# Query and key projections on column strips of TensorE, without padded weight copies

## The chip, the cores and the metric

The kernel runs on one core of a Trainium2 chip. A core has a matrix engine (TensorE, PE in the profile; its weight loads are listed apart as PEld), a vector engine (VectorE, DVE), an engine for functions of one variable (ScalarE, ACT), a general engine (GpSimd, POOL) and an engine that only issues transfers (SyncE, SP). Each works through its own list of instructions in order, and they wait for each other by semaphores. Operands lie in SBUF, 128 partitions wide; matmuls write to PSUM, eight banks of 128 x 512 fp32 numbers, from which DVE or ACT has to fetch the result ("evict" it). The metric is device time in microseconds (us), the median over several executions.

## The reference

Two layers are applied to x (2048 tokens, 448 features, bf16). Each is an attention block followed by a mixing block with an MLP, both on a normalised input:

```
qkv = layernorm(x) @ wqkv                 # 16 heads of 28 features each for q, k and v
p   = softmax(q @ k.T * 28**-0.5)
x   = x + (p @ v) @ wo
h   = gelu(layernorm(x') @ w1)            # x' = layernorm(x)
x1  = x' + shifted(h) @ w2                # four groups of features shifted by -1, +1, -2, +2 tokens
x   = x + x1 + gelu(layernorm(x1) @ w3) @ w4
```

Both layers share all weights.

## The kernel before

**Layout.** A head has 28 features, but TensorE's strips are 32 wide. So four heads form a group g (0 to 3) of 128 rows: head j of the group lies in rows 32j to 32j+27, and the four rows behind it hold helpers. `kT` and `qT` are kept in this way, transposed, with tokens along the free axis. Row 28 and row 29 of each head carry a bound on the scores, so that the exponential can run without a running maximum: rows 28 and 29 of K are 1 (the column `MK` adds them at eviction); row 28 of Q takes a multiple of the squared norm of the query, scaled by `ACOL`, and row 29 of Q a bias from the largest key norm. `ACOL` and `RTN` come from the norms of the weights themselves, which `wnorm` works out at the start: squares of the weights, column sums with a matmul by ones (L761), and sums over each head with a matmul by `astat` (L766).

**Weights of q and k.** `t_setup` loads them into `wst`, pieces of the later MLP buffer `h2T`, 112 features x 4 chunks x 448 columns. `pad_cast` then copies them to `wk_pad` and `wq_pad`, with each head's 28 columns at a multiple of 32 and zeros between: a copy for group 0 and two copies for groups 1 to 3, for each of the two (ACT at L741, or DVE at L743). `wnorm` squares the padded copies (ACT at L753, DVE at L755).

**Projections.** `kq_proj` makes 128 rows of K or Q for up to 512 tokens: four matmuls, one for each chunk of 112 features, with 128 padded columns as weights (L662); an eviction to `kT` or `qT` with a number as factor and, for K and later Q units, a column as addend (L930 to L937); squares of the result (L941, L943); and a matmul by `astat` that sums the squares over each head. `mm` gives every such matmul a second form, four matmuls on strips of 32 output columns (L665), which the planner takes when TensorE is already working in strips.

**Order.** Nothing is issued in the order of the source. Generators yield operations to a planner (`Sched`), which has a table of durations, due times from earlier rounds, and lists of seeds (`MOVES`) that disturb the due times at given points. It writes out a fixed order for every engine, and fills holes of TensorE with matmuls of ones (L1695). TensorE works in one of three tilings: scores on strips of 32 rows (L1252), products with V on strips of 32 columns (L1327, L665), and whole (L662, L872, L1695).

**Attention.** The scores of two or three blocks of 128 x 512 at a time (L1252) go through one exponential on ACT (L1278) of 1024 or 1536 columns; some blocks are taken to DVE instead (L1168 to L1181). The results meet V at L1327. Two score buffers of three banks alternate, so the scores of a step need the exponential two steps back. From the first exponential on, ACT is reserved for them, beside the tanh of the mixer (L1442) and the gelu of the MLP in nine batches (L1659). The first layer's projections of later tokens, the mixer, the MLP and the second layer's projections are laid between the scores. ACT evicts projections only before the first exponential.

Of the kernel before, what the change touches and what calls it, by code (L numbers as in the profile page):

```python
# [496 lines left out]
def build_kernel(nc, A_x, A_wqkv, A_wo, B_x, B_w1, B_w2, B_w3, B_w4, out, n_layers=2):  # L497
    S = A_x.shape[1]
    D = 448
# [21 lines left out]
            (0.00, 453789), (16.37, 681098), (32.56, 797911), (48.59, 756531), (64.60, 616122), (96.69, 243454), (112.73, 402327), (129.20, 347222),  # L521
            (193.55, 37042), (210.08, 918064), (242.29, 341149), (258.31, 397655), (274.47, 223313), (290.49, 246614), (306.70, 234581), (322.77, 119869),
            (338.97, 396652), (355.15, 335807), (391.48, 966107), (440.04, 112069), (520.56, 389665), (536.62, 623460), (552.63, 145884), (568.71, 985658),
            (584.75, 199060), (600.79, 794212), (620.06, 440366), (668.32, 428831), (700.60, 742412), (717.08, 172111), (733.21, 350167), (781.36, 465123),
            (797.48, 750518), (829.75, 99856), (845.88, 932005), (881.89, 550401), (898.03, 280990), (914.20, 779388), (946.64, 938909), (962.75, 215389),
            (978.81, 470403), (999.69, 102110), (1015.80, 600949), (1031.80, 257283),
        ],
        [
            (0.00, 913344), (12.07, 790630), (36.26, 358045), (48.38, 33421), (72.46, 243766), (96.67, 865488), (108.71, 222308), (145.54, 574177),
            (169.92, 505472), (194.21, 959135), (206.41, 140361), (218.93, 663650), (231.06, 874019), (255.76, 124206), (291.86, 733013), (328.10, 30459),  # L530
            (340.32, 970941), (364.69, 337305), (413.00, 152706), (425.18, 488991), (437.30, 939877), (449.57, 988047), (461.65, 669914), (473.72, 905087),
            (486.00, 87997), (498.03, 41039), (510.11, 162929), (522.19, 860735), (534.22, 735239), (546.27, 581631), (558.30, 115844), (570.45, 436555),
            (582.65, 408875), (606.74, 311018), (642.89, 325568), (667.19, 827655), (679.29, 868524), (691.61, 820707), (703.87, 927266), (716.12, 142611),
            (728.33, 661842), (752.69, 290694), (764.79, 914552), (776.96, 336386), (789.12, 558591), (801.16, 794121), (825.52, 153383), (849.92, 859691),
            (866.07, 319846), (878.17, 724156), (902.44, 789185), (914.49, 528957), (950.68, 252067), (974.81, 692424), (987.77, 461824), (1011.86, 320288),
            (1023.89, 587050), (1035.91, 787182), (1048.10, 662426),
# [40 lines left out]
    def c_act(n):  # L577
        return 0.08 + n * 0.000833
# [5 lines left out]
    with st:  # L584
        def sb(name, shape, dt):
            return st.enter_context(nc.sbuf_tensor(name, shape, dt))
# [25 lines left out]
        wq_pad = sb("wq_pad", [128, 4, 512], BF16)  # L612
        wk_pad = sb("wk_pad", [128, 4, 512], BF16)
# [32 lines left out]
        MK = cols[:, 4:5]  # L646
        ACOL, RTN, TMP, T2 = (sc[:, i, :] for i in range(4))
# [9 lines left out]
        def op(eng, dur, fn, reads=(), writes=(), **kw):  # L657
            return (eng, dur, fn, list(reads), list(writes), kw)
# [11 lines left out]
        def alt(eng, dur, fn, **kw):  # L670
            return (eng, dur, fn, kw)
# [17 lines left out]
        def t_setup():  # L689
            xin = A_x[0].rearrange("(t p) d -> p t d", p=128)  # L690
            wst = [h2T[:, 0:4, 0:D], h2T[:, 4:8, 0:D], wv]
            pads = ((wk_pad, "wk_pad"), (wq_pad, "wq_pad"))
# [5 lines left out]
            def ld_w(ci):  # L698
                return op("sp", 0.1, lambda e: e.dma_start(out=wst[ci][0:112, :, :], in_=A_wqkv[:, ci * D:(ci + 1) * D].rearrange("(c p) n -> p c n", p=112)),
                          writes=[("wst", ci)], dma=True, dma_time=(7.4, 6.4, 5.0)[ci])  # L700
# [15 lines left out]
            for (wp, nm) in pads:  # L716
                yield op("dve", 0.2, lambda e, wp=wp: e.memset(wp[:, :, :].rearrange("p c (h r) -> p c h r", r=32)[:, :, :, 28:32], 0.0), writes=[(nm, 0), (nm, 1)])
# [5 lines left out]
            yield op("dve", 0.15, lambda e: e.tensor_tensor(out=MK, in0=M28, in1=M29, op=ALU.add), reads=[("cols",)], writes=[(("cols",), 4)])  # L723
            yield ("sig", ("setup0",))
# [6 lines left out]
            def pad_cast(i, s):  # L731
                nm = pads[i][1]
                h0, h1 = ((0, 4), (4, 16))[s]
                nh = h1 - h0
                args = [(pads[i][0][0:112, :, 32 * h0:32 * h1].rearrange("p c (h r) -> p c h r", r=32)[:, :, :, 0:DH],
                         wst[1 - i][0:112, :, DH * h0:DH * h1].rearrange("p c (h r) -> p c h r", r=DH))]
                if s == 1:
                    args = [(a[:, 2 * k:2 * k + 2], z[:, 2 * k:2 * k + 2]) for a, z in args for k in range(2)]
                for k, (a, z) in enumerate(args):
                    n = 4 * DH * nh // len(args)  # L740
                    yield op("act", c_act(n), lambda e, a=a, z=z: e.activation(out=a, in_=z, func=ACT.Identity),  # L741
                             reads=[("wst", 1 - i)], writes=[((nm, s), k)],
                             alt=[alt("dve", c_b2b(n) + 0.1, lambda e, a=a, z=z: e.tensor_copy(out=a, in_=z))])  # L743

            def wnorm(s):
                gs = ((0,), (1, 2, 3))[s]
                ng = len(gs)
                lo, o = 128 * gs[0], 2 * gs[0]
# [3 lines left out]
                for i in range(2):  # L752
                    yield op("act", c_act(512 * ng), lambda e, i=i: e.activation(out=wsqs[i][0:112, :, lo:lo + 128 * ng], in_=pads[i][0][0:112, :, lo:lo + 128 * ng], func=ACT.Square),  # L753
                             reads=[(pads[i][1], s)], writes=[keys[i]],
                             alt=[alt("dve", c_f2b(512 * ng), lambda e, i=i: e.tensor_tensor(out=wsqs[i][0:112, :, lo:lo + 128 * ng], in0=pads[i][0][0:112, :, lo:lo + 128 * ng],  # L755
                                                                                            in1=pads[i][0][0:112, :, lo:lo + 128 * ng], op=ALU.mult))])
                b = yield ("acq", MISC, keys)
                for i in range(2):
                    for k, g in enumerate(gs):
                        for fc in range(4):  # L760
                            yield op("pe", 0.06, lambda e, fc=fc, i=i, k=k, g=g, b=b: e.matmul(  # L761
                                out=ps[:, bi(b), ng * i + k:ng * i + k + 1], lhsT=wsqs[i][0:112, fc, 128 * g:128 * g + 128], rhs=ones_bf[0:112, 0:1],
                                start=(fc == 0), stop=(fc == 3)),
                                reads=[keys[i], ("ones_bf",)], writes=[(("ps", bi(b)), ("c", i, g))], touch=[b])
                yield op("dve", 0.1, lambda e, b=b: e.tensor_copy(out=csum[:, o:o + 2 * ng], in_=ps[:, bi(b), 0:2 * ng]), reads=[("ps", bi(b))], writes=[("csum", s)], touch=[b])
                yield op("pe", 0.06, lambda e, b=b: e.matmul(out=ps[:, bi(b), 16:16 + 2 * ng], lhsT=astat[:, :], rhs=csum[:, o:o + 2 * ng], start=True, stop=True),  # L766
                         reads=[("csum", s), ("astat",)], writes=[(("ps", bi(b)), "h")], touch=[b])
# [17 lines left out]
            yield from pad_cast(0, 0)  # L785
            yield from pad_cast(1, 0)
# [3 lines left out]
            yield from pad_cast(0, 1)  # L790
            yield from pad_cast(1, 1)
# [131 lines left out]
        def kq_proj(xt, g, wpad, wnm, dst, dkeys, bias, bkey, nw, mul):  # L923
            b = yield ("acq", MISC, [xt.key, (wnm, min(g, 1))])
            for (fc, rows) in KCM:
                yield mm(nw, 128, lambda a, z, b=b: ps[a:z, bi(b), 0:nw], lambda a, z, fc=fc, rows=rows: wpad[0:rows, fc, 128 * g + a:128 * g + z],
                    xt.v[0:rows, 0:nw // 128, fc, :], fc == 0, fc == 3,
                    reads=[xt.key, (wnm, min(g, 1))], writes=[("ps", bi(b))], touch=[b])
            if bias is None:
                yield op("dve", 0.06 + c_ps(nw), lambda e, b=b: e.tensor_scalar(out=dst, in0=ps[:, bi(b), 0:nw], scalar1=mul, scalar2=None, op0=ALU.mult),  # L930
                         reads=[("ps", bi(b))], writes=dkeys, touch=[b],
                         alt=[alt("act", c_act(nw), lambda e, b=b: e.activation(out=dst, in_=ps[:, bi(b), 0:nw], func=ACT.Identity, scale=mul))])
            else:
                yield op("dve", 0.06 + c_ps(nw), lambda e, b=b: e.tensor_scalar(  # L934
                    out=dst, in0=ps[:, bi(b), 0:nw], scalar1=mul, scalar2=bias, op0=ALU.mult, op1=ALU.add),
                    reads=[("ps", bi(b)), bkey], writes=dkeys, touch=[b],
# [20 lines left out]
        def k_proj(L, c, g, xt):  # L957
            t0, n = KCH[L][c]
            c0, nw = kcol(L, t0), 128 * n
            b2 = yield from kq_proj(xt, g, wk_pad, "wk_pad", kT[:, g, c0:c0 + nw], [("kT", g, vslot(L, t0 + i)) for i in range(n)], MK, ("cols",), nw, 1.0)  # L960
# [5 lines left out]
        def q_proj(L, u, g, xt):  # L966
# [8 lines left out]
            b2 = yield from kq_proj(xt, g, wq_pad, "wq_pad", qt[:, g, q0:q0 + nw], wk, bias, bkey, nw, QS)  # L975
# [611 lines left out]
        def t_mixB(L, tiles, h0, batch, prio):  # L1587
# [18 lines left out]
            wstk = [("wst", 0), ("wst", 1), ("wsq",)]  # L1606
# [179 lines left out]
```

## Time and profile before

| what | value |
|---|---|
| median of 4 runs | 1063.4 us (1062.33 to 1066.47) |
| profiled execution | 1063.62 us |
| its span, first to last instruction | 1061.9 us |
| mean granted clock of TensorE | 0.995 |
| busy PE, ACT, DVE, POOL | 1023.4, 1016.2, 734.8, 58.8 us |
| matmuls in the trace | 9072 |
| first exponential, last exponential ends | 29.30, 1024.64 us |

A line of the timeline gives start and duration in us, engine, line of the source, operation, the tile written and the tiles read, shapes, how many instructions are merged in it, and in brackets how long the engine stood idle before and for whom. A line of a group gives the count after an x, the busy time, the mean duration in ns of one, and the idle time before them with what ended it. Durations of matmuls overlap: one of 512 columns lasts about 390 ns from end to end, but the next starts long before. So their pace is read from start to start.

### The profile page before, as it was taken

How to read it: one execution, taken by the hardware profiler on the slowest of the kernel's cores; microseconds unless marked ns; L12 is line 12 of the kernel's file. 1: busy time of each engine (PE TensorE's matmuls, PEld its weight loads, DVE VectorE, ACT ScalarE, POOL GpSimd, SP SyncE). 2: the span in 40 equal slices, each digit the busy share in tenths (PEclk: the TensorE clock that was granted, in tenths of full speed). 3: DMA queues.
4: the chain of work that ended last, by engine and by line, in shares of the span. 5: the costliest groups of instructions: out<-in, count | busy, mean ns of one | idle time of the engine just before them, and what ended most of it. 6: DMA issues, size and time to landing. Idle time of an engine off the chain costs nothing.

```text
span 1061.9 us, 21167 instructions
## 1 busy us (share of the span) xinstructions
PE 1023.4 (96%) x9072; PEld 398.1 (37%) x9072; DVE 734.8 (69%) x1685; ACT 1016.2 (96%) x938; POOL 58.8 (6%) x78
## 2 busy tenths in 40 slices
PE   9999999999999999999999999999999999999998
PEld 5333333333333333332343433333333333434455
DVE  7977478866887538887489656865869645665454
ACT  5999999999999999999999999999999999999983
POOL 1100000000000001010000000000011000010000
PEclk8999999999999999999999999999999999999999
DMA  4233141000001002100021002311010000000000
GB/s 115 60 111 100 35 122 20 2 16 20 21 1 21 1 1 41 35 21 1 21 41 31 26 15 77 90 31 40 21 36 2 20 14 19 22 21 2 15 6 23
DMA packets 70712, 35.04 MB, mean 33 GB/s; under 512 B 56473, under 2 KB 65049, under 8 KB 70617
## 3 DMA queue, kind: packets, MB, share of 16 engines
q1 hardware_dynamic: 70616, 33.68, 12.5%
q8 instruction: 71, 1.16, 0.4%
q14 instruction: 25, 0.20, 0.1%
HBM read 12.70 MB, written 7.08 MB: 19 GB/s over the span
## 4 chain that ended last, share of the span: by engine, by line
ACT 60%; PE 32%; DVE 5%; DMA 1%; issue 1%; POOL 0%; POOLq 0%; SPq 0%; DVEq 0%
ACT PT L1278 54%; PE ps L662 12%; PE ps L1252 8%; PE ps L1327 6%; ACT h2T L1659 4%; PE ps L1695 3%; PE ps L665 3%; ACT L1659 1%; DMA xT<-xn 1%; ACT gt L1442 1%; DMA h2T<-in_A_wqkv_dram 0%; ACT L1278 0%; DVE hT L1446 0%; DVE kT L934 0%; PE ps L872 0%
## 5 line engine op out<-in xcount | busy, mean ns | idle before, releaser
L1278 ACT ACTIVATE PT<-ps 128x1024 bf16<-128x1024 f32 (+1 forms) x821 | 916.7, 1221 | 10.0 <-PE ps L1252 6.9
L1252 PE MATMUL ps<-qT,kT 32*128 32x512 bf16 x1536 | 239.7, 384 | 11.7 <-ACT PT L1278 9.0
L1327 PE MATMUL ps<-PT,vaug 128*32 128x512 bf16 (+1 forms) x2253 | 233.6, 361 | 3.0 <-ACT PT L1278 1.9
L1695 PE MATMUL ps<-ones_bf 128*128 128x256 bf16 x1002 | 155.9, 280 | 2.0 <-DVE hot L696 1.1
L1252 PEld LDWEIGHTS ps<-qT,kT 32*128 32x128 bf16 x1536 | 58.8, 91 | 195.1 <-ACT PT L1278 104.9
L662 PE MATMUL ps<-xT,w 112*128 112x512 bf16 (+5 forms) x640 | 130.9, 327 | 0.8 <-DVE h2T L1618 0.6
L1695 PEld LDWEIGHTS ps<-ones_bf 128*128 128x128 bf16 x1002 | 83.5, 99 | 74.0 <-issue 55.2
L1618 DVE CAST h2T<-ps 128x512 bf16<-128x512 f32 (+2 forms) x126 | 73.5, 583 | 52.9 <-PE ps L662 41.8
L1327 PEld LDWEIGHTS ps<-PT,vaug 128*32 128x32 bf16 x2253 | 62.3, 94 | 112.0 <-issue 54.3
L1252 PE MATMUL ps<-kT 32*128 32x256 bf16 (+1 forms) x768 | 80.1, 310 | 3.6 <-ACT PT L1278 3.0
L662 PE MATMUL ps<-w,h2T 128*128 128x448 bf16 x299 | 70.3, 354 | 2.0 <-ACT h2T L1659 1.4
L662 PEld LDWEIGHTS ps<-xT,w 112*128 112x128 bf16 (+1 forms) x640 | 51.5, 104 | 52.4 <-issue 28.0
L1168 DVE TENSOR_SCALAR t<-ps 128x512 int32<-128x512 f32 x50 | 34.3, 686 | 31.4 <-PE ps L1252 31.0
L665 PE MATMUL ps<-w,h2T 128*32 128x448 bf16 x596 | 41.3, 366 | 5.6 <-ACT h2T L1659 3.9
L1252 PEld LDWEIGHTS ps<-kT 32*128 32x128 bf16 x768 | 21.4, 92 | 66.0 <-ACT PT L1278 35.4
L1659 ACT ACTIVATE h2T<-h2T 128x7168 bf16<-128x7168 bf16 (+2 forms) x9 | 44.8, 5010 | 0.1
L665 PE MATMUL ps<-xT,w 112*32 112x512 bf16 (+3 forms) x544 | 43.0, 334 | 0.0
L1577 POOL TENSOR_TENSOR mst<-mst,neghalf 128x1 f32<-128x1 f32 x32 | 25.2, 792 | 320.1 <-DVE mst L1575 318.2
L1356 DVE SCALAR_TENSOR_TENSOR uin<-uin,fct,ps 128x512 f32<-128x512 f32 x20 | 14.9, 743 | 35.8 <-PE ps L1327 35.7
L825 DVE BATCH_NORM_STATS2 st<-x_res 128x6 f32<-128x448 bf16 x64 | 38.6, 611 | 1.3 <-DMA x_res<-in_A_x_dram 0.9
L662 PEld LDWEIGHTS ps<-w,h2T 128*128 128x128 bf16 x299 | 24.8, 98 | 30.4 <-issue 11.4
L1479 POOL TENSOR_TENSOR mst<-mst,neghalf 128x4 f32<-128x4 f32 (+2 forms) x10 | 9.0, 906 | 473.2 <-DVE mst L1478 334.8
(149 smaller groups left out, 1095.9 us busy)
## 6 DMA issues: line engine op xcount, KB each, us to landing
uin<-uscr SPq DMA_DIRECT2D x20, 256.0 KB, 2.7
uscr<-u_sb SPq DMA_DIRECT2D x12, 256.0 KB, 2.0
uscr<-uin SPq DMA_DIRECT2D x8, 256.0 KB, 2.0
out_dram<-uin SPq DMA_DIRECT2D x16, 112.0 KB, 1.7
w<-in_B_w_dram SPq DMA_DIRECT2D x4, 392.0 KB, 3.9
x_res<-in_A_x_dram SPq DMA_DIRECT2D x3, 448.0 KB, 8.7
w<-in_B_w_dram SPq DMA_DIRECT2D x2, 448.0 KB, 6.4
h2T<-in_A_wqkv_dram SPq DMA_DIRECT2D x2, 392.0 KB, 5.6
```

Of the source, the lines that this page charges most:

```text
L662: return e.matmul(out=dst(0, m), lhsT=lhs(0, m), rhs=rhs, start=start, stop=stop)
L665: return [e.matmul(out=dst(a, min(m, a + 32)), lhsT=lhs(a, min(m, a + 32)), rhs=rhs, start=start, stop=stop, tile_position=(0, a)) for a i ...
L825: yield op("dve", 0.55, lambda e: e.bn_stats(out=st6[:, t, :], in_=x_res[:, t, :]), reads=[("x", t)], writes=[("st6", t)])
L1168: yield op("dve", 0.06 + c_ps(512), lambda e: e.tensor_scalar(out=t32[:, :], in0=ps[:, bk, :], scalar1=0.0, scalar2=65536.0, op0=ALU.max, ...
L1252: yield op("pe", 0.005 if ph == h else 0.012 + W / 2400.0, lambda e, bk=bk, r0=32 * j, g=g, kc=kc, qt=qt, q0=q0, W=W, c0=W * h: e.matmul(o ...
L1278: yield op("act", e_dur(n), lambda e, b0=b0, p0=p0, cnt=cnt: e.activation(out=PT[:, p0:p0 + cnt, :], in_=ps[:, b0:b0 + cnt, :], func=ACT.E ...
L1327: yield op("pe", nt * 0.054 if item in late else 0.004 + nt * 0.0133, lambda e, j=j, rhs=rhs, vs=vs, i=i: e.matmul(out=ps[32 * j:32 * j + ...
L1356: yield op("dve", 0.06 + c_ps(W), lambda e: e.scalar_tensor_tensor(out=uin[:, :], in0=uin[:, :], scalar=fct[:, L, k, g:g + 1], in1=ps[:, U ...
L1577: yield op("pool", 0.57, lambda e, t=t: e.tensor_tensor(out=mst[:, t, R3:R3 + 1], in0=mst[:, t, V3E:V3E + 1], in1=neghalf[:, 0:1], op=ALU. ...
L1618: yield op("dve", c_ps(NW), lambda e, fch=fch, b=b: e.tensor_copy(out=h2T[:, fch, hoff:hoff + NW], in_=ps[:, bi(b), 0:NW]), reads=[("ps", ...
L1659: yield op("act", c_act(14 * NW), lambda e, c0=c0, NW=NW: e.activation(out=h2T[:, :, c0:c0 + NW], in_=h2T[:, :, c0:c0 + NW], func=ACT.Gelu ...
L1695: SC.fill = (0.13, lambda e, b: e.matmul(out=ps[:, bi(b), 0:256], lhsT=ones_bf[:, :], rhs=ones_bf[:, :].unsqueeze(1).to_broadcast([128, 2, ...
```

## The change

- The weights of q and k are loaded to tiles of their own, `wq_raw` and `wk_raw`, in the layout of the input, with eight zero columns behind the last head. `wq_pad`, `wk_pad`, `pad_cast` and the zeroing of the padding are gone.
- `kq_proj` issues, for each chunk of features, four matmuls on strips of 32 columns, one per head, each with weights from column 28 x head to 28 x head + 31. The last four columns of a strip are the first four of the next head, so rows 28 to 31 of each head receive numbers that don't belong there.
- The eviction multiplies by a column instead of a number: `ONE28` (1 in the first 28 rows of a head, 0 in the others) for K, `QS28` (the same times the score factor) for Q. This clears these rows.
- `wnorm` squares the raw weights, 112 columns for a group instead of 128, and sums over heads with a new 0/1 tile `a28` that maps 28-row heads to 32-row ones. Two operations on GpSimd make it, two on VectorE make the columns.
- The planner is given other seeds (`MOVES`), so the order of all engines is written anew.
- In `t_mixB`, `h2T` no longer waits for readers of the weights that used to lie there.

```diff
-        wq_pad = sb("wq_pad", [128, 4, 512], BF16)
-        wk_pad = sb("wk_pad", [128, 4, 512], BF16)
+        wq_raw = sb("wq_raw", [112, 4, 456], BF16)
+        wk_raw = sb("wk_raw", [112, 4, 456], BF16)
+        a28 = sb("a28", [112, 128], BF16)
...
-            for (wp, nm) in pads:
-                yield op("dve", 0.2, lambda e, wp=wp: e.memset(wp[:, :, :].rearrange("p c (h r) -> p c h r", r=32)[:, :, :, 28:32], 0.0), writes=[(nm, 0), (nm, 1)])
+            for ci in range(2):
+                yield op("dve", 0.1, lambda e, ci=ci: e.memset(raw[ci][:, :, D:D + 8], 0.0), writes=[(("wst", ci), "p")])
+            for k in range(2):
+                yield op("pool", 0.3, lambda e, k=k: e.affine_select(out=a28[:, :].rearrange("p (j r) -> p j r", r=32), in_=(a28, ones_bf)[k == 0][0:112, 0:128].rearrange("p (j r) -> p j r", r=32),
+                                                                pattern=[[(28, -28)[k == 0], 4], [0, 32]], compare_op=ALU.is_ge, fill=0.0, base=(27, 0)[k == 0], channel_multiplier=(-1, 1)[k == 0]),
+                         reads=[("ones_bf",), ("a28",)], writes=[("a28",)])
...
+            yield op("dve", 0.2, lambda e: e.reduce_max(out=ONE28, in_=astat[:, :], axis=AX.X), reads=[("astat",)], writes=[(("cols",), 5)])
+            yield op("dve", 0.15, lambda e: e.tensor_scalar(out=QS28, in0=ONE28, scalar1=QS, scalar2=None, op0=ALU.mult), reads=[("cols",)], writes=[(("cols",), 6)])
...
-            yield from pad_cast(0, 0)
-            yield from pad_cast(1, 0)
             yield ("spawn", wnorm(0), 0)
             if GATE3:
                 yield ("wait", GATE3)
-            yield from pad_cast(0, 1)
-            yield from pad_cast(1, 1)
             yield ("spawn", wnorm(1), 1)
...
-        def kq_proj(xt, g, wpad, wnm, dst, dkeys, bias, bkey, nw, mul):
-            b = yield ("acq", MISC, [xt.key, (wnm, min(g, 1))])
+        def kq_proj(xt, g, w, wkey, dst, dkeys, bias, bkey, nw, mul):
+            b = yield ("acq", MISC, [xt.key, wkey])
             for (fc, rows) in KCM:
-                yield mm(nw, 128, lambda a, z, b=b: ps[a:z, bi(b), 0:nw], lambda a, z, fc=fc, rows=rows: wpad[0:rows, fc, 128 * g + a:128 * g + z],
-                    xt.v[0:rows, 0:nw // 128, fc, :], fc == 0, fc == 3,
-                    reads=[xt.key, (wnm, min(g, 1))], writes=[("ps", bi(b))], touch=[b])
+                yield op("pe", c_mm(nw) + Sched.COLT, lambda e, b=b, fc=fc, rows=rows: [e.matmul(
+                    out=ps[32 * j:32 * j + 32, bi(b), 0:nw], lhsT=w[0:rows, fc, DH * (4 * g + j):DH * (4 * g + j) + 32],
+                    rhs=xt.v[0:rows, 0:nw // 128, fc, :], start=fc == 0, stop=fc == 3, tile_position=(0, 32 * j)) for j in range(4)],
+                    reads=[xt.key, wkey], writes=[("ps", bi(b))], touch=[b], mode="col4")
...
-            b2 = yield from kq_proj(xt, g, wk_pad, "wk_pad", kT[:, g, c0:c0 + nw], [("kT", g, vslot(L, t0 + i)) for i in range(n)], MK, ("cols",), nw, 1.0)
+            b2 = yield from kq_proj(xt, g, wk_raw, ("wst", 1), kT[:, g, c0:c0 + nw], [("kT", g, vslot(L, t0 + i)) for i in range(n)], MK, ("cols",), nw, ONE28)
...
-            b2 = yield from kq_proj(xt, g, wq_pad, "wq_pad", qt[:, g, q0:q0 + nw], wk, bias, bkey, nw, QS)
+            b2 = yield from kq_proj(xt, g, wq_raw, ("wst", 0), qt[:, g, q0:q0 + nw], wk, bias, bkey, nw, QS28)
```

## The prediction

> **What bounds the kernel now.** I read the busy shares first, then the groups of costly instructions.
>
> ```profile
> PE 1023.4 (96%) x9072; PEld 398.1 (37%) x9072; DVE 734.8 (69%) x1685; ACT 1016.2 (96%) x938; POOL 58.8 (6%) x78
> ...
> L1278 ACT ACTIVATE PT<-ps 128x1024 bf16<-128x1024 f32 (+1 forms) x821 | 916.7, 1221 | 10.0 <-PE ps L1252 6.9
> ...
> L1695 PE MATMUL ps<-ones_bf 128*128 128x256 bf16 x1002 | 155.9, 280 | 2.0 <-DVE hot L696 1.1
> ```
>
> TensorE (PE) and ScalarE (ACT) both show 96%, but 1002 of PE's matmuls are fillers of ones (L1695) that nobody reads, so PE has slack; the 821 exponentials of L1278 have none: only 10.0 us of waiting stands before them. Next the busy time in three stretches, cut at the first and last exponential (columns: stretch, length, then busy time and count for PE, PEld, DVE, ACT, POOL; PE clock; DMA).
>
> ```profile
> 0.00:29.30 29.30, 26.84 (x167) 14.41 (x167) 21.41 (x87) 16.31 (x24) 7.02 (x18) 0.88 0.38 105
> 29.30:1024.64 995.34, 963.56 (x8583) 362.30 (x8582) 694.43 (x1554) 984.03 (x876) 46.73 (x53) 1.00 0.13 31
> 1024.64:1061.90 37.26, 32.97 (x324) 21.44 (x324) 18.92 (x47) 15.87 (x39) 5.02 (x7) 1.00 0.05 17
> ```
>
> So the span is a head of 29.30 us, a middle of 995.34 us in which ACT works 984.03 and rests 11.3, and a tail of 37.26 us. An early first exponential is worth its full gain if the middle doesn't give it back.
>
> The head, from the timeline (start, duration, instruction, count, idle before):
>
> ```profile
> 7.44 0.76 ACT L917 ACTIVATE xn<-x_res,vpe,rstd 128x448 bf16<-128x448 bf16 x1 [3.87 <-DVE vpe L915]
> ...
> 8.11 1.40 ACT L741 ACTIVATE wk_pad<-h2T 112x672 bf16<-112x672 bf16 x2
> ...
> 9.41 0.61 ACT L753 ACTIVATE h2T<-wk_pad 112x512 bf16<-112x512 bf16 x1
> ...
> 9.94 1.40 ACT L741 ACTIVATE wq_pad<-h2T 112x672 bf16<-112x672 bf16 x2
> ...
> 11.24 0.74 ACT L917 ACTIVATE xn<-x_res,vpe,rstd 128x448 bf16<-128x448 bf16 x1
> 11.89 0.61 ACT L753 ACTIVATE w<-wq_pad 112x512 bf16<-112x512 bf16 x1
> 12.41 0.74 ACT L917 ACTIVATE xn<-x_res,vpe,rstd 128x448 bf16<-128x448 bf16 x1
> ...
> 14.16 1.89 PE L662 MATMUL ps<-xT,wk_pad 112*128 112x512 bf16 x4 [0.28 <-DVE wsum L768]
> ...
> 28.70 0.60 PE L1252 MATMUL ps<-qT,kT 32*128 32x512 bf16 x5
> 29.30 4.62 ACT L1278 ACTIVATE PT<-ps 128x1536 bf16<-128x1536 f32 x4
> ```
>
> ACT is full from 7.44 to 13.15. Four pad copies (L741) stand ahead of its last two normalised tiles (L917), and the first K projection (14.16) needs the last of them. From there PE and the evictions set the pace until the first scores (28.70).
>
> **The change, part by part.** Sums are against the profiled execution: 1063.62 us, span 1061.9, so 1.7 lie around the span; the median of the runs is 1063.4, 0.2 lower.
>
> *Copies out, squares smaller.* ACT loses two pairs of 1.40. DVE loses two copies of 0.28. In the changed order ACT squares 1344 columns of wk, then one tile, 448 columns of wq, two tiles. The 0.61 of 512 columns at L753 and a slope of 0.83 ns a column (1460 less 1037 ns for 512 more in L1278) give 1.30 and 0.56. The wk load is there at 6.99, when DVE's copy could start: 7.0+1.30=8.3, tile to 9.0, wq square to 9.4 (its load was there at 8.46), two tiles to 10.7. The last tile ended at 13.15, and 1.0 later K began; so K begins at about 11.8: **-2.35**. DVE's new squares (448 and 1344 columns; 1536 took 0.95) replace two of 0.95 and end by 9.4, ahead of its last tile copies. Loads, their order and their queue (SP) are the same four DMAs; the two at issue only land in another tile.
>
> *Added set-up.* Two affine selects on POOL (0.30 each by the one at L707), before its power at 6.07; a reduction and a scaling on DVE (0.4 together by L721 to L723 and the wider input) after 2.5, before x lands at 3.36; two smaller memsets for two of 0.17. All hidden: 0; without the cover 0.4.
>
> *K and Q as strips.* 304 products: 248 were plain and 56 strips already. The trace has both forms side by side:
>
> ```profile
> 47.73 0.82 PE L665 MATMUL ps<-xT,wk_pad 112*32 112x512 bf16 x8
> 48.17 0.61 PE L1327 MATMUL ps<-PT,vaug 128*32 128x512 bf16 x7
> ...
> 53.52 0.82 PE L662 MATMUL ps<-xT,wk_pad 112*128 112x512 bf16 x3
> 54.27 0.39 PE L1252 MATMUL ps<-qT,kT 32*128 32x512 bf16 x3
> ```
>
> Eight strips, two sets of four, hold PE 0.44, or 0.22 a set; three plain ones 0.75, of which 0.10 is the turn to another tiling: 0.217 each. A set costs what one matmul does. Against this stands the Trainium skill ("TensorE: Matmul & The Clock Gate", Part 3, measured speedup): three column strips brought 2.38 and four row strips 3.07 times, not 3 and 4, so a set would be 4/3.07=1.30 matmuls. By it 248 sets add 248 x 0.065=16 us of PE, by the row 248 x 0.003, under 1. I take the row. Strips now begin at odd multiples of 56 bytes, which no row shows: 0 if their loads stay hidden behind 0.22, up to the skill's 16 if not; I take 0, since the load beside each set is small.
>
> *Order.* The built order of the changed kernel has 1762 turns between tilings against 1741: 21 x 0.10=2.1 us of PE, beside 74 fewer fillers (74 x 0.109=8.1, a filler being 256 columns at half of 0.217). ACT's list from the first exponential on has the same counts of every form, so its 984.03 stay.
>
> *Evictions.* K and Q now scale by a column, not a number. On ACT a column costs 0.09 (L937 with one 687 ns, L932 with none 597); on DVE 0.06 (L934 749, L930 682). DVE: 65 x 0.06=3.9 us, under a DVE with 300 us free: 0, at most 1 where K is awaited. ACT, in the head: two banks pass between PE and ACT every 0.86 to 0.9 us per group, so seven slower evictions cost 7 x 0.09/2=**+0.3**.
>
> *Rest of the head.* Before, ten groups of four lie between the second square sum and the first scores; after, nine (one K group moved behind them): **-0.87**; one more square sum stands there: **+0.2**. Then the clock:
>
> ```profile
> 13.72:20.55 6.83, 6.48 (x25) 2.44 (x22) 3.98 (x20) 1.91 (x3) 1.41 (x2) 0.50 0.01 1
> 20.55:29.30 8.75, 8.74 (x45) 3.13 (x42) 8.51 (x28) 5.92 (x10) 2.87 (x5) 1.00 0.00 0
> ```
>
> PE ran at half rate from 13.72 to 20.55, where some 11 products of 512 columns lay: 11 x 0.216=2.4 us. PE was busy for 0.67 to 0.8 of each us before that, with short transposes and column sums. The skill (same page, Part 1) says the rate falls after an idle window of about 3.4 us and is back after a busy one. By it a K projection from 11.8 on fills the window and the whole 2.4 goes; by the row, which fell without an idle window, K and Q of the first group escape but as many later sets fall in: 0. I take about half: **-1.1**.
>
> Head: -2.35+0.3-0.87+0.2-1.1=-3.8, first exponential near 25.5.
>
> *Middle.* ACT waits where PE has a long stretch between two groups of scores:
>
> ```profile
> 558.34 2.37 ACT L1278 ACTIVATE PT<-ps 128x1536 bf16<-128x1536 f32 x2 [1.61 <-PE ps L1252]
> ```
>
> Before that wait 32 strips stood in a row. Counting the orders with the durations above, stretches over 1.8 us between score groups are 23 before and 28 after, the longest (gelu and ends left out) 2.78 and 2.61. More of them, none worse: **+0.2**, bounds -3 and +4. *Tail*: the same instructions with 4 fewer fillers; 0, within 1.
>
> Sum: -3.6, or 1063.4-3.6=**1059.8 us**.
>
> **Rivals.** *The gain is larger* (1056.2): the clock never falls (-1.3 beyond the half) and sets placed among the strips of L1327 need no turn, so the middle's 11.3 us of waits shrink by a fifth (2.3 us). For: 371 and 377 turns now go between strips and scores, fewer to plain; against: more turns in all.
>
> *The middle gives it back* (1063.1): five more long stretches at 11.3/23=0.5 us are 2.5, and DVE's slower evictions 1. For: DVE is 81% busy from 29.3 to 100 us (57.13 of 70.70), where K is awaited. Against: K is needed some 30 us ahead there.
>
> *Slower* (1071): a set costs the skill's 1.30. Exposed are the 24 sets on the head's path, the 70 plain K and Q products in the layer change from 370 to 600 us, where PE paces ACT, and half of the other 154: 171 x 0.065=11.1 on -3.6, so 1063.4+7.5. The sign turns once a set costs 3.6/171=0.021 us over a matmul. Against it stand the strips above.
>
> *No effect of the copies*: if K's start hung on the 49 fillers that hold PE until 9.2 or on the loads, not on ACT, the -2.35 would go, leaving 1062.1; the waits above speak for ACT.
>
> **How the numbers follow.** This kernel's times tell about 0.3% (3.2 us) from nothing, so faster is under 1060.2 and slower over 1066.6. My forecast has 0.62 (0.38 under 1060.2, 0.24 same; its own range 1057 to 1062.5, from the clock, 0 to 2.4, and the middle), the larger gain 0.17 (0.16 faster), the gain given back or the copies off the path 0.12 (0.11 same, 0.01 slower), the slower one 0.09. Sums: faster 0.54, same 0.36, slower 0.10. The range from 1055.5 to 1065.5 takes in the larger gain and the gain given back, and leaves out the slower case and the ends.
>
> **What would show it.** K's first strips near 11.8 us, the first exponential at 24 to 27, ACT's busy time after it 984, its waits 11 with bounds 8 to 15, a tail of 37, and eight-strip runs of 0.44. Wrong would be: the head unchanged; strips at 0.28 a set; or ACT waits before L1269 (the exponential's new line) that grow by more than the head wins.

## The result, and the profile after

The changed kernel takes 1060.85 us (median, 1057.06 to 1063.36), the kernel before 1064.0 in the runs beside it. The ratio of the two is 0.9965, with a 95% interval from 0.9956 to 0.9974: about 3.7 us, or 0.35%. The prediction said 1059.8, a gain of 3.6.

The execution that was profiled lies at the upper end of that spread: 1063.36 us with a span of 1061.6, hardly under the 1061.9 of the kernel before. So this profile must be read piece by piece, not by its end. The busy shares, and the two groups of instructions whose lines before are in the prediction:

```profile
PE 1026.6 (97%) x9883; PEld 397.4 (37%) x9883; DVE 744.9 (70%) x1686; ACT 1015.6 (96%) x933; POOL 57.7 (5%) x80
...
L1269 ACT ACTIVATE PT<-ps 128x1024 bf16<-128x1024 f32 (+1 forms) x821 | 917.8, 1225 | 11.6 <-PE ps L1243 7.8
...
L1686 PE MATMUL ps<-ones_bf 128*128 128x256 bf16 x928 | 144.0, 279 | 2.6 <-DVE hot L698 1.1
```

PE has 811 more matmul records (a set of strips counts as four) and 3.2 us more busy time; ACT is as full as it was. The same three stretches as in the prediction, cut at the first exponential and at the end of the last:

```profile
0.00:26.94 26.94, 24.34 (x289) 13.76 (x289) 19.74 (x84) 14.39 (x19) 7.58 (x20) 0.94 0.42 114
26.94:1024.96 998.02, 970.27 (x9279) 362.02 (x9278) 706.63 (x1557) 985.16 (x875) 45.40 (x53) 0.99 0.14 32
1024.96:1061.60 36.64, 32.00 (x316) 21.67 (x316) 18.54 (x46) 16.09 (x39) 4.77 (x7) 1.00 0.05 17
```

The head is 2.36 us shorter (26.94 against 29.30) and the tail 0.62 (36.64 against 37.26), but the middle is 2.68 longer (998.02 against 995.34). Its granted clock of 0.99 says where to look. Two stretches of this execution ran with PE at half rate (third figure from the end), one in the head and a long one in the middle:

```profile
12.60:16.00 3.40, 3.40 (x35) 1.16 (x33) 1.25 (x7) 0.78 (x1) 0.55 (x1) 0.50 0.06 20
695.20:712.30 17.10, 16.59 (x114) 4.01 (x111) 11.46 (x25) 14.04 (x13) 0.00 (x0) 0.50 0.14 32
```

In the second, ACT worked 14.04 of 17.10 us: PE at half rate couldn't feed it, and ACT stood idle for 3.06 us. In the middle of the kernel before, the profile has only one such stretch, of 3.4 us at 986.5.

The head, first ACT's part of the timeline:

```profile
7.81 1.32 ACT L748 ACTIVATE h2T<-wk_raw 112x1344 bf16<-112x1344 bf16 x1 [4.23 <-DMA wk_raw<-in_A_wqkv_dram]
9.04 0.75 ACT L907 ACTIVATE xn<-x_res,vpe,rstd 128x448 bf16<-128x448 bf16 x1
9.69 0.56 ACT L748 ACTIVATE w<-wq_raw 112x448 bf16<-112x448 bf16 x1
10.15 1.40 ACT L907 ACTIVATE xn<-x_res,vpe,rstd 128x448 bf16<-128x448 bf16 x2
...
26.94 1.45 ACT L1269 ACTIVATE PT<-ps 128x1536 bf16<-128x1536 f32 x1 [0.16 <-PE ps L1243]
```

The copies are gone, and the last tile ends at 11.55 where it ended at 13.15. But ACT now starts with the squares of wk (L748), and these waited for the load until 7.81. Then PE's part:

```profile
12.66 1.90 PE L916 MATMUL ps<-xT,wk_raw 112*32 112x512 bf16 x16
14.34 1.85 PE L916 MATMUL ps<-xT,wq_raw 112*32 112x512 bf16 x16
...
26.50 0.60 PE L1243 MATMUL ps<-qT,kT 32*128 32x512 bf16 x5
27.04 0.62 PE L916 MATMUL ps<-xT,wk_raw 112*32 112x512 bf16 x8
27.48 0.39 PE L668 MATMUL ps<-sq,astat 128*32 128x512 bf16 x4
```

K's first strips start at 12.66. They and Q's fall into the half-rate stretch, so sixteen strips take 1.7 us instead of the 0.87 of four sets at full clock. Once the clock is full, eight strips take 0.44 from start to start (27.04 to 27.48), as they did before.

### The profile page after: what moved, and what is told of

It reads as the page before. It is cut to its first block, busy times and chain, and to the rows that moved or that the text cites. A ratio compares the mean times of both kernels' runs of the same rounds, so it can differ in the third digit from the quotient of the medians.

```text
span 1061.6 us, 22787 instructions
## 1 busy us (share of the span) xinstructions
PE 1026.6 (97%) x9883; PEld 397.4 (37%) x9883; DVE 744.9 (70%) x1686; ACT 1015.6 (96%) x933; POOL 57.7 (5%) x80
## 3 DMA queue, kind: packets, MB, share of 16 engines
q1 hardware_dynamic: 70616, 33.68, 13.6%
## 4 chain that ended last, share of the span: by engine, by line
ACT 53%; PE 41%; DVE 4%; DMA 1%; issue 1%; SPq 0%; POOLq 0%; POOL 0%; DVEq 0%
ACT PT L1269 46%; PE ps L1243 11%; PE ps L1318 9%; PE ps L665 9%; PE ps L1686 5%; ACT h2T L1650 4%; PE ps L916 3%; PE ps L668 3%; ACT L1650 1%; ACT gt L1433 1%; ACT L1269 1%; DMA wk_raw<-in_A_wqkv_dram 1%; DMA xT<-xn 0%; DVE kT L925 0%; DVE h2T L1609 0%
## 5 line engine op out<-in xcount | busy, mean ns | idle before, releaser
L1318 PE MATMUL ps<-PT,vaug 128*32 128x512 bf16 (+1 forms) x2253 | 251.4, 364 | 2.1 <-ACT PT L1269 1.4
L1686 PE MATMUL ps<-ones_bf 128*128 128x256 bf16 x928 | 144.0, 279 | 2.6 <-DVE hot L698 1.1
L1318 PEld LDWEIGHTS ps<-PT,vaug 128*32 128x32 bf16 x2253 | 65.8, 94 | 118.4 <-issue 66.5
L1686 PEld LDWEIGHTS ps<-ones_bf 128*128 128x128 bf16 x928 | 77.6, 99 | 71.6 <-issue 50.3
L665 PE MATMUL ps<-w,h2T 128*128 128x448 bf16 x327 | 75.1, 354 | 4.8 <-ACT h2T L1650 3.5
L668 PE MATMUL ps<-xT,w 112*32 112x512 bf16 (+4 forms) x612 | 51.5, 337 | 0.0
L916 PE MATMUL ps<-xT,wq_raw 112*32 112x512 bf16 (+1 forms) x576 | 47.4, 371 | 0.8 <-DVE qT L921 0.3
L1340 DVE STREAM_TRANSPOSE u_sb<-ps 128x512 f32<-128x512 f32 (+1 forms) x24 | 15.0, 626 | 40.9 <-PE ps L1318 40.9
L916 PE MATMUL ps<-xT,wk_raw 112*32 112x512 bf16 (+3 forms) x640 | 41.8, 346 | 0.3 <-DVE xT L867 0.2
L665 PEld LDWEIGHTS ps<-w,h2T 128*128 128x128 bf16 x327 | 27.9, 98 | 35.1 <-issue 11.7
```

The costliest lines, as they stand in the source:

```text
L665: return e.matmul(out=dst(0, m), lhsT=lhs(0, m), rhs=rhs, start=start, stop=stop)
L668: return [e.matmul(out=dst(a, min(m, a + 32)), lhsT=lhs(a, min(m, a + 32)), rhs=rhs, start=start, stop=stop, tile_position=(0, a)) for a i ...
L916: yield op("pe", c_mm(nw) + Sched.COLT, lambda e, b=b, fc=fc, rows=rows: [e.matmul(out=ps[32 * j:32 * j + 32, bi(b), 0:nw], lhsT=w[0:rows, ...
L1318: yield op("pe", nt * 0.054 if item in late else 0.004 + nt * 0.0133, lambda e, j=j, rhs=rhs, vs=vs, i=i: e.matmul(out=ps[32 * j:32 * j + ...
L1686: SC.fill = (0.13, lambda e, b: e.matmul(out=ps[:, bi(b), 0:256], lhsT=ones_bf[:, :], rhs=ones_bf[:, :].unsqueeze(1).to_broadcast([128, 2, ...
```

## Experiments

Two theories stood at the start. Mine: the gain comes from ACT's copies in the head, strips cost nothing, the middle gives nothing back. The rival: the order that was written anew, with its other seeds, or the evictions by a column move the time as much as the copies do. Each run below stands beside runs of the kernel before from the same comparison; where times from different comparisons are set against each other, this is said.

### The changed kernel again

Nothing is edited.

> The changed kernel once more, for a second trace with its clock. Theory (the head is shorter by 3 to 4 us and the rest is as before): first exponential at 24 to 27 us, ACT waits after it 8 to 13 us where the clock stays full, ratio to before 0.9965 within 0.001. Rival (the middle gives part of a larger head gain back at full clock too): waits of 13 us or more in this trace as well.

Measured: 1060.05 us against 1063.2, ratio 0.9954 (0.993 to 0.9979). The profile of this run has the same mean clock as the profile of before, 0.995, so the two can be laid side by side. Its three stretches:

```profile
0.00:26.39 26.39, 24.24 (x288) 14.07 (x289) 19.83 (x84) 14.40 (x20) 7.60 (x20) 0.94 0.45 117
26.39:1022.39 996.00, 963.35 (x9266) 361.69 (x9278) 706.11 (x1557) 984.69 (x875) 45.47 (x53) 1.00 0.14 32
1022.39:1059.00 36.61, 31.99 (x316) 21.64 (x316) 18.53 (x46) 16.12 (x39) 4.77 (x7) 1.00 0.05 17
```

Against before: head -2.91, middle +0.66, tail -0.65, span -2.9. At like clock the gain is in the head, and the middle keeps nearly all of it. ACT rests 11.3 us in the middle (996.00 less 984.69), as before and within the 8 to 13 expected.

These runs show how much the clock weighs. Over twelve runs the time of the changed kernel follows its mean granted clock: 1056.9 and 1057.3 us at 1.000, 1057.6 to 1058.1 at 0.998, 1060.3 to 1060.8 at 0.995, 1063.5 at 0.990. A straight line through them meets clock 1 at 1057.0 us and loses 0.64 us for each 0.001. The kernel before, over 23 runs, meets clock 1 at 1059.5 and loses 0.81. A half-rate stretch is 3.4 us long or a multiple of it, and 3.4 us at half rate take 3.4 x 0.5/1060=0.0016 from the mean clock: 1.0 us for the changed kernel, 1.3 for the one before. So by these lines 2.5 of the 3.15 us between the medians are there at full clock. The other 0.65 go with the difference in clock (0.9962 in the mean of these runs against 0.9946, about one stretch less in each). The lines show that time and clock go together; they don't by themselves say which makes the other.

### The copies put back

ACT's four copies of 672 columns return to the changed order, two after the first tile and two after the square of wq, with nobody reading what they write.

```diff
+        acts = P.ops["act"]
+        for k, (i, z) in enumerate(((2, wk_raw), (5, wq_raw))):
+            for h in range(2):
+                at = acts[i + h]
+                o = _Op("act", lambda e, h=h, k=k, z=z: e.activation(
+                    out=h2T[0:112, 4 * k + 2 * h:4 * k + 2 * h + 2, 0:384].rearrange("p c (h r) -> p c h r", r=32)[:, :, :, 0:DH],
+                    in_=z[:, 2 * h:2 * h + 2, 112:448].rearrange("p c (h r) -> p c h r", r=DH), func=ACT.Identity), False)
+                o.pos = at.pos
+                acts.insert(i + h + 1, o)
```

> The changed kernel, its written-out order kept, with four copies of 672 columns put back on ACT in the head (raw weights of groups 1 to 3 to a free part of h2T that nobody reads), one pair behind the first tile, one behind the second square. Theory (the copies stood on the path): the last tile and the first exponential come 4 x 0.65 = 2.6 us later, and so does the end: ratio to before 0.999 (0.998 to 1.000). Rival (the gain comes from the new order, or the middle absorbs an earlier start): the end moves by less than 1 us, ratio 0.9965 to 0.9975.

Measured: 1064.21 us, ratio 1.0005 (0.999 to 1.0019), so 4.2 us over the changed kernel of the experiment above, which ran beside it, and the whole gain is gone. This is more than the 2.6 us that were expected. ACT's timeline of the head:

```profile
8.46 0.74 ACT L907 ACTIVATE xn<-x_res,vpe,rstd 128x448 bf16<-128x448 bf16 x1
9.11 1.40 ACT L1725 ACTIVATE h2T<-wk_raw 112x672 bf16<-112x672 bf16 x2
10.41 0.56 ACT L748 ACTIVATE w<-wq_raw 112x448 bf16<-112x448 bf16 x1
10.88 1.40 ACT L1725 ACTIVATE h2T<-wq_raw 112x672 bf16<-112x672 bf16 x2
12.19 1.40 ACT L907 ACTIVATE xn<-x_res,vpe,rstd 128x448 bf16<-128x448 bf16 x2
```

The last tile ends at 13.59, and K's first strips start at 15.46. PE has meanwhile lost its clock, for three times as long as in the changed kernel (one window of the trace):

```profile
11.20:21.40 10.20, 8.45 (x72) 4.68 (x76) 4.20 (x20) 4.48 (x7) 1.41 (x2) 0.50 0.21 73
```

The first exponential comes at 30.16. In the profile of that kernel, without the copies, the last tile ended at 11.43, with a load that landed 0.45 later: the copies themselves delay the chain by 2.6 us. The first exponential is 3.8 us later than in that profile, and the longer half-rate stretch accounts for the rest as far as the trace shows. A line through the runs meets clock 1 at 1060.3, so 3.3 us over the changed kernel, but none of these runs had a clock above 0.995, and the line is drawn out beyond them. So the copies were on the path, and "no effect of the copies" falls. The reverse, copies taken out of the kernel before with its order kept, was not run.

### The seeds of one kernel in the other

Only the lists of `MOVES` are exchanged: the changed kernel with the seeds of before, and the other way round.

```diff
     MOVES = [
         [
-            (0.00, 797926), (16.57, 107192), (32.60, 709727), (64.94, 836138), (81.19, 737549), (97.22, 243454), (113.42, 815160), (129.90, 480401),
+            (0.00, 453789), (16.37, 681098), (32.56, 797911), (48.59, 756531), (64.60, 616122), (96.69, 243454), (112.73, 402327), (129.20, 347222),
...
```

> The changed kernel with the seeds of the kernel before, so another order of all engines. Theory (the head's gain comes from the removed copies, whatever the seeds): still faster than before, 0.995 to 0.999. Rival (the new seeds make the gain): 1.000 or more.

> The kernel before with the seeds of the changed one. Theory: the padded copies still stand in the head, so 0.999 to 1.004. Rival (the seeds make the gain): 0.9965 or less.

Measured: 1106.72 us, ratio 1.0403 (1.0369 to 1.0437), and 1101.73 us, ratio 1.0364 (1.033 to 1.0398). Each kernel loses some 40 us with the seeds of the other. I had missed this wholly: I took seeds to be worth a few us. ACT's longest lines in the list of its waits, of the changed kernel with the seeds of before:

```profile
ACT PT L1269 <- PE ps L1243: 38.4, 46, 3.9
ACT gt L1433 <- DVE gw L1422: 8.4, 9, 3.1
```

The exponentials wait 38.4 us for scores, in the changed kernel 7.8. Neither seed list is worth anything with the other list of operations: both times are worse than those without any seeds below. So exchanged seeds don't divide this change into two parts, and the next pair has none.

### Both kernels without seeds

```diff
     MOVES = [
...
-    ]
+    MOVES = [[], []]
```

> The changed kernel with no seeds at all, so the planner's own order. Theory (the change is worth some 3 us in any order, but an order is worth tens): 1.03 to 1.08 of before; earlier than the kernel before without seeds by 2 to 6 us. Rival (the change helps or harms by the order that it allows): the two without seeds differ by over 10 us, either way.

> The kernel before with no seeds. Theory: 1.03 to 1.08, and 2 to 6 us later than the changed kernel without seeds. Rival: over 10 us apart, either way.

Measured: the changed kernel 1084.9 us, ratio 1.0188 (1.0141 to 1.0235); the kernel before 1092.76, ratio 1.0262 (1.0215 to 1.0309). The edit is worth 7.9 us here, between the theory's 2 to 6 and the rival's 10, but from two runs each, and at clocks of 0.992 and 0.997 against 0.989 and 0.984. A line through each pair meets clock 1 at 1081.4 and 1084.0, 2.6 us apart, as with seeds; two points make that no more than a hint. In the traces the first exponential comes at 20.21 against 23.26, and the middle takes 1026.19 against 1027.64. So the head is some 3 us shorter in this order too (one half-rate stretch of 3.4 us against 6.8 among them), and seeds are worth another 25 to 30 us to either kernel.

### Evictions by a column, alone

In the kernel before, the number at the eviction of K and Q becomes a column; the order stays.

```diff
+            col = ones_f[:, 0:1] if mul == 1.0 else cols[:, 6:7]
...
-                    out=dst, in0=ps[:, bi(b), 0:nw], scalar1=mul, scalar2=bias, op0=ALU.mult, op1=ALU.add),
+                    out=dst, in0=ps[:, bi(b), 0:nw], scalar1=col, scalar2=bias, op0=ALU.mult, op1=ALU.add),
```

> The kernel before, its order kept, with the factor of every K and Q eviction read from a column of ones or of the score factor instead of a number (one more memset on DVE at the start makes the second column). Theory (the slower evictions are hidden but for the head): 0.0 to +0.5 us, ratio 1.000 to 1.001; L934 with two columns 0.81 us against 0.75. Rival (they hold up the middle where PE waits for K and Q): +1 to +3 us, ratio 1.001 to 1.003.

Measured: 1068.13 us against 1065.85, ratio 1.0027 (1.001 to 1.0045): the rival's +1 to +3, not my 0 to 0.5. DVE's groups by form:

```profile
L935 DVE TENSOR_SCALAR kT<-ps,ones_f,cols 128x512 bf16<-128x512 f32 x20 | 16.0, 809 | 10.6 <-PE ps L662 10.1 <-PE ps L665 0.4
...
L931 DVE TENSOR_SCALAR qT<-ps,cols 128x512 bf16<-128x512 f32 x8 | 5.9, 742 | 1.7 <-PE ps L662 1.6
```

With one column in place of a number the eviction of L931 takes 742 ns (682 before). That of L935 has two columns where it had one, and takes 809 (749 before). DVE is busy for 3.5 us more (738.3 against 734.8), near the 3.9 of the prediction. On the clock line, however, this kernel meets clock 1 at 1061.2, only 0.6 over the 1060.6 of the runs beside it. The rest goes with the mean clock, 0.9911 against 0.9927. Its profile has half-rate stretches at 108.4 us (10.2 us long) and 152.7 (3.4), where the profile of the kernel before has none. Whether the later evictions bring these about, the runs don't tell.

### One whole matmul for four strips

The changed order, with each set of four strips replaced by one matmul on 128 raw columns. A head's rows then don't lie at multiples of 32; the time per instruction is what counts.

```diff
-                yield op("pe", c_mm(nw) + Sched.COLT, lambda e, b=b, fc=fc, rows=rows: [e.matmul(
-                    out=ps[32 * j:32 * j + 32, bi(b), 0:nw], lhsT=w[0:rows, fc, DH * (4 * g + j):DH * (4 * g + j) + 32],
-                    rhs=xt.v[0:rows, 0:nw // 128, fc, :], start=fc == 0, stop=fc == 3, tile_position=(0, 32 * j)) for j in range(4)],
+                yield op("pe", c_mm(nw) + Sched.COLT, lambda e, b=b, fc=fc, rows=rows: e.matmul(
+                    out=ps[:, bi(b), 0:nw], lhsT=w[0:rows, fc, 104 * g:104 * g + 128],
+                    rhs=xt.v[0:rows, 0:nw // 128, fc, :], start=fc == 0, stop=fc == 3),
```

> The changed kernel, its order kept, with each set of four strips replaced by one whole matmul on 128 raw columns (so heads don't fall on multiples of 32 and the outputs are not the reference's). Theory (a set costs what a matmul does): the pace of a set, 0.22, is that of the matmul, and the added turns between tilings cost PE some 0.1 us each but little of the end: 0 to +3 us against the changed kernel, ratio to before 0.996 to 0.999. Rival (a set costs 1.3 matmuls): 304 products give PE 20 us back and the end comes 2 to 5 us earlier: 0.992 to 0.995.

Measured: 1066.47 us, ratio 1.0012 (0.999 to 1.0033): slower than with strips, by more than I had expected. At clock 1 its runs meet 1063.1, 2.5 us over the 1060.6 of the kernel before beside them; the strips lay 2.5 us under theirs in another comparison. So whole matmuls cost some 5 us in this order. There the products lie among other work in strips, and whole ones add turns of the tiling: counted in the built order, 1856 against 1762, and 94 x 0.10 is 9.4 us of PE. The traces, in which a few matmuls are missing, show 1848 turns against 1753, and PE is busy for 1027.5 us against 1019.6 in the profile of "The changed kernel again", at the same mean clock of 0.995. It shows in the waits of the exponentials for scores, here first the changed kernel of that profile:

```profile
ACT PT L1269 <- PE ps L1243: 6.3, 14, 1.6
```

and here whole matmuls:

```profile
ACT PT L1269 <- PE ps L1243: 10.1, 24, 1.6
```

If a set of strips cost 1.30 matmuls, the 304 sets would have saved PE 304 x 0.065=19.8 us against these 9.4, and the waits would have shrunk. They grew, and that rival falls. That the turns make all of the 5 us isn't shown.

### The half-rate stretch in the middle

In two profiles of the changed kernel PE fell to half rate near 700 us. It is not full there: in the 9.2 us ahead of the first of these falls it worked 7.85, and waited once for an eviction to kT (0.46 us) and twice for exponentials (0.4 each). So the score matmuls of nineteen exponentials from about 686 to 703 us were issued twice, to keep it full, and in a second kernel those of seven.

```diff
-                        rhs=qt[r0:r0 + 32, g, q0:q0 + W], start=True, stop=True, tile_position=(r0, 0)),
+                        rhs=qt[r0:r0 + 32, g, q0:q0 + W], start=True, stop=True, tile_position=(r0, 0)) for _ in range(1 + (550 <= n < 569))],
```

> The changed kernel, its order kept, with the score matmuls of 19 exponentials (about 686 to 703 us) issued twice, the second over the first with the same values, so that PE is busier where it waits for evictions of Q. Theory (PE's clock falls to half near 700 us because PE is idle there, and that costs 3 us in most runs): no half rate between 690 and 720, the end 1 to 3 us earlier than the changed kernel, ratio to before 0.993 to 0.9955. Rival (the fall is not set by PE's use there, or costs nothing since ACT paces): the same as the changed kernel or later by what the added matmuls take, up to 19 x 0.22 = 4 us, ratio 0.9965 to 1.000.

Measured with nineteen: 1060.23 us, ratio 0.9954 (0.9936 to 0.9972). The profile has no half-rate stretch at all; the window in question:

```profile
686.00:703.00 17.00, 15.51 (x182) 4.23 (x176) 15.29 (x27) 16.20 (x15) 0.00 (x0) 1.00 0.19 46
```

PE is now busy for 15.51 of 17 us and the mean clock over the runs is 0.998. But at clock 1 the kernel takes 1059.2, where the changed one took 1057.0 in another comparison; the kernel before differs by 1.1 between the two (1060.6 and 1059.5), so 1 to 2 us of this are the doubled matmuls. ACT stands idle for 0.8 us in this window. What is won by the clock is about paid for in matmuls. The kernel with seven, with `556 <= n < 563` in the line above, ran with the changed kernel beside it:

> The changed kernel, its order kept, with the score matmuls of only 7 exponentials (about 691 to 698 us) issued twice. Theory (the added matmuls cost what they hold PE, the fall of the clock 3 us in most runs): no half rate between 690 and 720 in most runs, and 1 us less paid for it than with 19: 0.5 to 1.5 us earlier than the 19, 1 to 2.5 us earlier than the changed kernel of the same call. Rival: the fall comes as often as in the changed kernel, and the end is the same within 1 us.

> The changed kernel beside the one with doubled scores, on the same chip. Theory: ratio to before 0.995 to 0.998; a half-rate stage near 700 us in most runs.

Measured with seven: 1059.78 us, ratio 0.9961 (0.9943 to 0.9979). The changed kernel beside it: 1056.98 us (1056.75 to 1058.79), ratio 0.9929 (0.9902 to 0.9957). So the doubled scores were 2.8 us slower, not faster. At clock 1 they are 0.8 slower (1057.7 against 1056.9); the rest goes with their lower clock, 0.9968. There was little to win: this time the unchanged kernel itself hardly lost its clock, 0.9992 in the mean, against what was expected of it. Its profile has no half-rate stretch before the last 3 us, and is the clean picture of the change:

```profile
0.00:24.84 24.84, 22.65 (x288) 13.56 (x289) 20.16 (x84) 14.40 (x20) 7.58 (x20) 1.00 0.46 124
24.84:1018.34 993.50, 960.93 (x9266) 361.71 (x9278) 706.12 (x1557) 984.25 (x876) 45.40 (x53) 1.00 0.14 32
1018.34:1055.00 36.66, 32.00 (x316) 21.66 (x316) 18.54 (x46) 16.09 (x39) 4.76 (x7) 0.99 0.05 17
```

It also takes my reason for the fall away. The stretch in which the first profile fell, and the one ahead of it, from this trace:

```profile
686.00:695.20 9.20, 7.26 (x90) 2.42 (x83) 8.23 (x16) 9.17 (x9) 0.00 (x0) 1.00 0.11 30
695.20:712.30 17.10, 15.06 (x186) 5.72 (x186) 16.00 (x36) 17.09 (x16) 0.00 (x0) 1.00 0.20 47
```

PE was less busy ahead of it than where it fell (7.26 against 7.85), and kept its clock. ACT worked 17.09 of 17.10 us where it had worked 14.04. The same program on the same data falls in one execution and not in the next, so the holes alone don't decide it. Between them the three profiles also show the effect of the clock on the time, with nothing else changed: 17.1, 6.8 and 0 us of half rate in the middle, which lasted 998.02, 996.00 and 993.50 us.

### PE kept full in the head

Eight more fillers go between the transposes and column sums ahead of K's first strips, and three that stand before the second square sum are issued twice.

```diff
+        pes = P.ops["pe"]
+        for o in pes[108:111]:
+            o.fn = lambda e, f=o.fn: [f(e), f(e)]
+        for i in (97, 79, 73, 60):
+            at = pes[i]
+            for k in range(2):
+                o = _Op("pe", lambda e: SC.fill[1](e, "b3"), False)
+                o.pos = at.pos
+                pes.insert(i + 1, o)
```

> The changed kernel's order with PE's holes in the head filled: eight more matmuls of ones of 256 columns between the transposes and column sums that precede the first K strips, and the three that stand before the second square sum issued twice. Nothing else differs. Theory (half-rate stages of PE cost the head 1 to 3 us, and come where PE is only partly busy): no stage at half rate between 10 and 20 us, first exponential at 24.8 to 25.5 us, the middle as it was, ratio to the kernel before 0.992 to 0.9955. Rival (the stage follows the load of the transposes and sums or is set by something else than PE's holes, or the added matmuls delay the first K strips): a half-rate stage as before or K strips from 12.8 us on, first exponential at 26 to 27.5 us, ratio 0.9955 to 0.998.

Measured: 1059.62 us against 1064.64, ratio 0.9947 (0.9928 to 0.9966). PE's timeline of the head:

```profile
12.40 0.38 PE L1686 MATMUL ps<-ones_bf 128*128 128x256 bf16 x2
12.71 1.05 PE L916 MATMUL ps<-xT,wk_raw 112*32 112x512 bf16 x16
13.59 1.04 PE L916 MATMUL ps<-xT,wq_raw 112*32 112x512 bf16 x16
```

There was no half-rate stretch between 10 and 20 us: sixteen strips took 0.88. The first exponential came at 25.44. Both are as the theory said, and so is the ratio. But this doesn't show that the fillers did it. The changed kernel without them also kept its clock there in one of three profiles, with an exponential at 24.84, and so did the kernel with nineteen doubled scores, whose head is the same. The mean clock over the runs is 0.9967, about that of the changed kernel (0.9962), since this kernel still falls later: in its profile for 10 of the 13.6 us from 693. And at clock 1 it takes 1057.5, which is 2.5 under the 1060.0 of the kernel before beside it: the gain that the changed kernel has without the fillers. So it isn't shown to be a better version.

## Why the prediction was right

**The sum.** A gain of 3.6 us was worked out, and the ratio says 3.7. At full clock 2.5 to 3.0 us are left (1059.5 and 1057.0 in one comparison, 1059.8 and 1056.9 in another); the prediction had 2.5 without its clock term. That the sums agree to 0.1 us is luck in part: the copies gave less than forecast in most profiles, the tail gave 0.6 that wasn't forecast, and the clock's share of the median changed from one comparison to the next.

**Copies out (-2.35).** The right mechanism, as the copies put back show, with a size that depends on the execution. K's strips came at 12.66, 12.52 and 12.11 in the three profiles of the changed kernel, not at 11.8: -1.50 to -2.05 against 14.16. What was off is "the wk load is there at 6.99". It landed at 7.81, 7.68 and 7.28. From there the chain was as worked out, 3.74 us to the end of the last tile against 3.7, and K followed 1.1 later. The kernel with seven doubled scores has the same head, and in its profile the load landed early. First ACT's line, then PE's:

```profile
7.02 1.32 ACT L748 ACTIVATE h2T<-wk_raw 112x1344 bf16<-112x1344 bf16 x1 [3.44 <-DMA wk_raw<-in_A_wqkv_dram]
```

```profile
11.88 1.90 PE L916 MATMUL ps<-xT,wk_raw 112*32 112x512 bf16 x16
```

There K began at 11.88, 0.1 from the forecast. So the full -2.35 is there when the load lands at 7.0, and a later load takes its delay from it. Before, the first thing ACT did was a tile, which needed no weights; now the squares are first in its queue, so a late load moves everything behind it. Why the load lands at 7.0 in one execution and at 7.8 in another, the runs don't tell.

**From K to the first exponential (+0.3, -0.87, +0.2 and the clock's -1.1).** 15.14 us became 14.28 and 13.87 in the two profiles of the changed kernel with one half-rate stretch of 3.4 us, and 12.73 in that with none. The prediction had 13.67, and 12.37 had the whole 2.4 of the clock gone. So the sum comes out 0.2 to 0.6 us too low in each case, and which of its terms is short isn't known. Half the clock was a fair middle: of two half-rate stretches in a row (6.8 us) one stayed, or none.

**Strips (0).** They hold at 0.22 us a set also from weights that begin at odd multiples of 56 bytes. The traces decide against the 1.30, which was the prediction's estimate from a page's speedups.

**Evictions (0, at most 1).** The size on DVE was right (+0.06 us, 3.5 us in all), and by the clock lines it costs the end 0.6 us. The rest of the +2.3 measured for that change alone went with its clock.

**Middle (+0.2) and tail (0).** At full clock the middle was 993.50 us, at like clock 996.00, in the profile with the long fall 998.02: -1.8, +0.7 and +2.7 against before, within the bounds of -3 and +4. But those bounds were drawn from stretches between scores, and what moved the middle was the clock; ACT's own busy time stayed within 1.2 us of 984.03. The tail came out 0.6 shorter in all three profiles. I can't say by which of its instructions. The copies put back leave it at 36.66 us and columns in the kernel before at 37.25, so neither of these two edits explains it; the rewritten order may.

**The rivals.** "The middle gives it back" happened in the execution that was profiled first, but through the clock, not through longer stretches between scores or slower evictions. The slower case (strips at 1.30) and "no effect of the copies" were refuted above. "The larger gain" came in one comparison, where the changed kernel took 1056.98, and by its first part: the clock hardly fell (0.9992).

## What to carry over

Work on the path ahead of a steady state is worth its length, less what the shortened queue then waits for: ask what its first instruction needs. In this kernel a seed list was good only for the operations that it was found for, so compare two edits each with an order of its own, or both with none. And when a kernel's times spread by half a per cent, plot them against the granted clock before explaining a difference of that size, and compare only with runs of the same comparison: here the same kernel before met clock 1 anywhere from 1059.5 to 1060.6.

## What was not expected of the hardware

PE fell to half rate in the middle of a steady stretch without any long idle time: it was busy for 7.85 of the 9.2 us before, and its longest wait there was 0.46 us. The prediction quoted the Trainium skill ("TensorE: Matmul & The Clock Gate", Part 1) for a rule by which an idle window of about 3.4 us comes first; no such window is in this trace. The lengths of the falls in these traces, 3.4 us or a multiple of it (6.8, 10.2, 17.1), fit a window of that size. By the clock line of the changed kernel, 3.4 us at half rate go with 1.0 us of its time. What starts a fall stays open: the same program fell at 695 us, at 702, or not at all.
